# Attention with a gated feed-forward layer: four score banks for the first four pairs, and the first weights' high halves rounded on ScalarE

## The chip, the cores and the metric

The program runs on one NeuronCore of a Trainium2 chip. The metric is the device time of one execution, in microseconds (us); the median of three runs of the kernel before is 751.47 us (749.72 to 752.3). TensorE (PE in the profile) multiplies matrices into PSUM, VectorE (DVE), ScalarE (ACT) and GpSimd (POOL) work on vectors, and SyncE (SP) issues the transfers. Each engine takes its instructions in the order in which they stand in its own queue.

## The reference

Causal attention of 4 batches, 8 heads, 576 tokens and 64 dimensions per head is mixed with a linear memory. Its output, 2304 tokens of 512 features, goes through a gated feed-forward layer ("experts" in the kernel) with 1536 hidden features:

```python
scores = scale * np.matmul(q, k.transpose(0, 1, 3, 2))
scores = np.where(causal, -1000000000.0, scores)
a = softmax(scores);  local = np.matmul(a, v)
q_p = phi(q)                                  # elu(q) + 1
mem_out = (q_p @ M_prev) / (q_p @ z_prev + 1e-6)
attn = g * mem_out + (1 - g) * local          # g: a gate for each head
x = attn.transpose(0, 2, 1, 3).reshape(2304, 512)
out = (silu(x @ w_gate) * (x @ w_val)) @ w_out
```

The weights come as 64-bit floats; everything is asked for in 32-bit precision.

## The kernel before

The 32 pairs of batch and head are handled two heads at a time: 16 "pairs", four to a batch. A pair's `load` brings q and k, `split` parts each into a rounded high half and the rest (`qh`, `ql`, `kh`, `kl`), and a score tile is the sum of three matmul products of these. `scores(t, ...)` makes the tile of 128 queries number t (0 to 3) against the 128(t+1) keys before them, for both heads, one PSUM bank for each head; `scores4` makes the last 64 queries of both heads in two halves of 288 keys, one bank each. From a bank VectorE takes the masked, scaled copy and the row minimum in one instruction (L406, L428), ScalarE the exponential and its sum (L410, L433), GpSimd divides (`weighed`, L449), TensorE transposes (L473, L493), VectorE and ScalarE in turn copy the transposes out (L318, L320), TensorE multiplies with the values (L548, L602) and adds the memory's part (L463, L464), and `give` (L518, L519) writes the pair's features as a high and a low half, which L630 stores to a scratch array in DRAM, `xdh` and `xdl`. The first five pairs (`PLAIN`) keep the attention weights and the values in plain 32 bits, without halves.

PSUM has eight banks here: two for scores (`s`), three for transposes (`tr`), one for the products with values (`av`), one (`g`) and one (`m`) for the experts. `rot` hands out the buffers of a name in turn. Before the two matmul series of a tile write their banks, they wait until the last reader of the second bank is done (L402).

The experts' weights are 12 groups f of 128 hidden features, each in thirds (gate, value, out) of 128 x 512. For each third `weights` loads the raw 64-bit words (L170, two buffers in turn for the first groups), turns them into 32-bit floats in four instructions (L176 on ScalarE, L177, L179, L180 on VectorE; one buffer each for the results `e` and `a`), rounds the high half `wh` (L184 on ScalarE for the groups with the tag "b", L107 on GpSimd for those with the tag "a"), and takes the low half `wl` as the difference (L111, on GpSimd for "a"). Groups 0 to 3, tag "a", are 12 thirds; they are converted beside the first pairs. The other eight groups have the tag "b" and come later.

`moe1` multiplies the first 1536 tokens with groups 0 to 3, 256 tokens at a time, beside the attention of pairs 4 to 15. It loads a slice of `xdh` and `xdl` (L193, L194), which needs the four pairs of a batch stored. What is left is done after the attention, by L203, L212 to L214, L737 to L744.

The code gives each step a priority, and a scheduler places every instruction in its engine's queue by these priorities and by its own estimate of when the operands are there. So an edit of buffers or engines also moves instructions that it does not name. In the first stretch the code gives the steps of pair n and of pair n-1 in the order of `STEPS`.

Of the kernel before, what the change touches and what calls it, by code (L numbers as in the profile page):

```python
# [9 lines left out]
F32 = mybir.dt.float32  # L10
# [28 lines left out]


PLAIN = tuple(range(0, 5))
EV = (1, 2)
P_X = -400
ORDER = (4, 5, 0, 1, 2, 3)
HI_ACT = ('b',)
ACT_K = (0, 1)
N4 = 1
ON_POOL = ("wa", "q", "k")
PS_S, PS_T, PS_A, PS_G, PS_M = 2, 3, 1, 1, 1
# [11 lines left out]
def attention_moe(ctx: ExitStack, tc: tile.TileContext, qt, kt_, v, m, beta, wg, wv, wo, out):  # L61
# [5 lines left out]
    psS = ctx.enter_context(tc.tile_pool(name="psS", bufs=1, space=PSUM))  # L67
# [27 lines left out]
    def rot(pool, name, shape, dtype, n):  # L95
        held = slots.setdefault(name, [0, []])
        if len(held[1]) < n:
            held[1].append(pool.tile(shape, dtype, name=f"{name}{len(held[1])}"))
        held[0] += 1
        return held[1][(held[0] - 1) % n]  # L100
# [160 lines left out]
    with tc.tile_pool(name="sb", bufs=1, reuse_waits="tile") as sb:  # L261
# [48 lines left out]
                SP.dma_start(mm[rows, :, j, :], m[b, rows])  # L310
            return mm

        turn = [0]

        def evac(dst, src):
            turn[0] += 1
# [7 lines left out]
        class Pair:  # L324
# [62 lines left out]
            def scores(self, t, c):  # L387

                w = 128 * (t + 1)
                mx = self.mx  # L390
                ps = [rot(psS, "s", [128, 512], F32, PS_S) for _ in range(2)]
                last = None
                for i, (q, k) in enumerate(self.products):
                    for h in range(2):
                        rows = slice(h * 64, h * 64 + 64)
                        mm = PE.matmul(  # L396
                            ps[h][:, 0:w], q[rows, t * 128 : t * 128 + 128], k[rows, 0:w], start=(i == 0), stop=(i == 2)
                        )
                        if last is not None:
                            follow(mm, last, "the two heads' products take turns")  # L400
                        elif id(ps[1]) in read:
                            follow(mm, read[id(ps[1])], "once both banks are read", mybir.DependencyClass.Sync)  # L402
                        last = mm
                for h in range(2):
                    p = rot(sb, "pl", [128, 512], F32, NBIG) if t > 1 else rot(sb, "ps", [128, 256], F32, NSMALL)
                    read[id(ps[h])] = DVE.tensor_tensor_reduce(  # L406
                        out=p[:, 0:w], in0=ps[h][:, 0:w], in1=maskp[:, 512 - w : 512], op0=ALU.add, op1=ALU.min,
                        scale=-SCALE, scalar=BIG, accum_out=mx[:, c + h : c + h + 1],
                    )
                    ACT.activation(  # L410
                        p[:, 0:w], p[:, 0:w], AF.Exp, bias=mx[:, c + h : c + h + 1], scale=-1.0,
                        accum_out=self.sm[:, c + h : c + h + 1],
                    )
                    self.pts[(t, h)] = p

            def scores4(self):
# [4 lines left out]
                p = p4s[self.n % N4]  # L421
                mx = self.mx
                for half in range(2):
                    ps = rot(psS, "s", [128, 512], F32, PS_S)
                    sl = slice(half * 288, half * 288 + 288)
                    for i, (q, k) in enumerate(self.products):
                        PE.matmul(ps[:, 0:288], q[:, 512:640], k[:, sl], start=(i == 0), stop=(i == 2))
                    read[id(ps)] = DVE.tensor_tensor_reduce(  # L428
                        out=p[:, sl], in0=ps[:, 0:288], in1=mask4 if half else maskp[:, 0:288], op0=ALU.add, op1=ALU.min,
                        scale=-SCALE, scalar=BIG if half == 0 else mx[:, c : c + 1],  # L430
                        accum_out=mx[:, c + half : c + half + 1],
                    )
# [376 lines left out]
```

## Time and profile before

| | us |
|---|---|
| median of three runs | 751.47 |
| the profiled execution | 753.47 |
| its span, first to last instruction | 751.7 |
| TensorE busy | 693.1 (92%) |
| VectorE busy | 401.7 (53%) |
| ScalarE busy | 332.4 (44%) |
| GpSimd busy | 197.9 (26%) |
| mean clock that TensorE was granted | 0.966 |

The profile gives, for groups of instructions by line, how long they took, how long their engine stood idle just before them and what ended that idle time; a view by stretches of the span gives each engine's busy time and TensorE's granted clock; a timeline shows single instructions, with the idle time before each and what ended it in square brackets. The shares over the whole span say little about single stages: TensorE is nearly always busy after the first 125 us, GpSimd is idle after the attention. Line numbers are those of the kernel before; in the changed kernel they are higher by one from `WIDE` on and by seven from `evac` on (L396 is L403 there, L184 is L185).

### The profile page before, as it was taken

To read this page: it belongs to the slowest core of one execution; us is meant where nothing else is said; L and a number is where in the kernel's file an instruction comes from. 1 tells how busy PE (TensorE), PEld (TensorE's weight loads), DVE (VectorE), ACT (ScalarE), POOL (GpSimd) and SP (SyncE) were. 2 spreads that over 40 slices of the span, in tenths; PEclk is the share of its full clock that TensorE was granted. 3 is DMA by queue.
4 is the path that set the end of the run, shared out by engine and by line. 5 is a ranking of instruction groups with operands and counts; after the bars stand their busy time and mean duration, and the time that the engine had idled before them with its cause. 6 is when DMAs were issued, how large, how long until landed. Compare 5 with 4: busy or idle time off the path is not lost.

```text
span 751.7 us, 11326 instructions
## 1 busy us (share of the span) xinstructions
PE 693.1 (92%) x4172; PEld 621.6 (83%) x4172; DVE 401.7 (53%) x1042; ACT 332.4 (44%) x737; POOL 197.9 (26%) x264
## 2 busy tenths in 40 slices
PE   4577798999979999899969999999999999999997
PEld 2466676998769997698859999999999999999996
DVE  8887764776876977775736995111111221211212
ACT  5555455667668686576725663211121111111111
POOL 5885943544444553452300000000000000000000
PEclk9789799999989999899988999999999999999999
DMA  9555144230362312401048760300040310400201
GB/s 262 180 169 148 54 124 150 70 114 19 104 197 88 114 39 78 162 33 61 20 156 295 221 226 26 115 1 1 13 156 1 112 57 0 169 1 1 84 1 43
DMA packets 43928, 72.58 MB, mean 97 GB/s; under 512 B 11744, under 2 KB 24544, under 8 KB 43872
## 3 DMA queue, kind: packets, MB, share of 16 engines
q1 hardware_dynamic: 43728, 71.56, 29.4%
q8 instruction: 33, 0.54, 0.3%
q10 hardware_dynamic: 144, 0.29, 0.1%
q14 instruction: 23, 0.19, 0.1%
HBM read 54.54 MB, written 17.30 MB: 96 GB/s over the span
## 4 chain that ended last, share of the span: by engine, by line
PE 70%; DVE 11%; DMA 8%; ACT 6%; issue 2%; POOL 2%; SPq 0%; DVEq 0%; ACTq 0%; POOLq 0%
PE s L203 13%; PE g L203 9%; PE m L203 8%; PE av L203 6%; PE tr L213 5%; PE tr L212 5%; PE tr L214 5%; PE s L396 3%; PE av L616 2%; PE tr L473 2%; DMA xbl<-xdl 2%; PE av L602 2%; PE m L212 2%; DMA xbh<-xdh 1%; PE m L213 1%
## 5 line engine op out<-in xcount | busy, mean ns | idle before, releaser
L743 ACT CAST uh<-u 128x384 fp32r<-128x384 f32 x56 | 28.8, 514 | 109.8 <-DVE u L738 109.8
L213 PE MATMUL tr<-wl,uh 128*128 128x512 f32 x168 | 66.5, 396 | 0.0
L212 PE MATMUL tr<-wh,uh 128*128 128x512 f32 x168 | 66.1, 393 | 0.0
L214 PE MATMUL tr<-wh,ul 128*128 128x512 f32 x168 | 64.7, 396 | 0.0
L738 DVE SCALAR_TENSOR_TENSOR u<-s,u 128x384 f32<-128x384 f32 x23 | 12.8, 557 | 86.9 <-PE s L203 86.9
L396 PE MATMUL s<-kh,qh 64*128 64x128 f32 (+3 forms) x128 | 31.1, 463 | 28.8 <-DVE mx L406 15.2
L410 ACT ACTIVATE pl<-pl,mx 128x384 f32<-128x384 f32 (+1 forms) x64 | 42.6, 667 | 31.3 <-DVE mx L406 31.2
L449 POOL TENSOR_SCALAR pl<-pl,rs 128x384 f32<-128x384 f32 (+1 forms) x64 | 44.4, 712 | 19.9 <-ACT x L500 10.8
L396 PEld LDWEIGHTS s<-kh,qh 64*128 64x128 f32 x128 | 14.0, 207 | 40.3 <-DVE mx L406 18.6
L111 DVE TENSOR_TENSOR ul<-u,uh 128x384 fp32r<-128x384 f32 x56 | 31.2, 557 | 26.7 <-ACT uh L743 26.7
L111 DVE TENSOR_TENSOR g2l<-tr,g2h 128x512 fp32r<-128x512 f32 (+1 forms) x66 | 36.2, 572 | 17.1 <-ACT g2h L455 16.4
L449 POOL TENSOR_SCALAR ps<-ps,rs 128x128 f32<-128x128 f32 (+1 forms) x64 | 27.9, 454 | 61.2 <-DVE rs L446 26.4
L473 PE MATMUL tr<-ident,pl 128*128 128x128 f32 x224 | 39.9, 316 | 3.5 <-POOL pl L449 2.0
L406 DVE CUSTOM_DVE_ANT_0 pl<-s,maskp 128x384 f32<-128x384 f32 (+1 forms) x64 | 37.7, 618 | 9.9 <-PE s L396 9.9
L473 PEld LDWEIGHTS tr<-ident,pl 128*128 128x128 f32 x224 | 29.3, 161 | 10.4 <-POOL pl L449 4.5
L214 PEld LDWEIGHTS tr<-wh,ul 128*128 128x128 f32 x168 | 31.6, 188 | 7.3
L203 PE MATMUL s<-xbh,wh 128*128 128x384 f32 x92 | 32.1, 352 | 4.9 <-DMA xbh<-xdh 4.9
L212 PEld LDWEIGHTS tr<-wh,uh 128*128 128x128 f32 x168 | 31.6, 188 | 5.2
L213 PEld LDWEIGHTS tr<-wl,uh 128*128 128x128 f32 x168 | 31.6, 188 | 5.1
L410 ACT ACTIVATE ps<-ps,mx 128x128 f32<-128x128 f32 (+1 forms) x64 | 28.9, 452 | 13.3 <-DVE mx L406 13.1
L455 ACT CAST g2h<-tr 128x512 fp32r<-128x512 f32 (+1 forms) x66 | 30.5, 494 | 7.0 <-PE tr L473 4.8
L737 ACT ACTIVATE u<-s 128x384 f32<-128x384 f32 x23 | 11.2, 489 | 49.5 <-PE s L203 49.5
(197 smaller groups left out, 2188.2 us busy)
## 6 DMA issues: line engine op xcount, KB each, us to landing
qr<-in_qt_dram SPq DMA_DIRECT2D x16, 384.0 KB, 4.2
out_dram<-pt SPq DMA_DIRECT2D x18, 256.0 KB, 2.2
kr<-in_kt_dram SPq DMA_DIRECT2D x15, 288.0 KB, 3.8
xdh<-xh SPq DMA_DIRECT2D x15, 288.0 KB, 2.6
xdl<-xl SPq DMA_DIRECT2D x15, 288.0 KB, 2.2
wrawb<-in_wg_dram SPq DMA_DIRECT2D x8, 512.0 KB, 4.1
wrawb<-in_wv_dram SPq DMA_DIRECT2D x8, 512.0 KB, 4.4
wrawb<-in_wo_dram SPq DMA_DIRECT2D x8, 512.0 KB, 4.3
```

The lines of the kernel that those rows point to most:

```text
L111: return eng.tensor_tensor(dst, src, hi.bitcast(F32), op=ALU.subtract)
L203: PE.matmul(ps, wt[:, c], xx[:, kk, :], start=(n == 0), stop=(n == 11))
L212: PE.matmul(ps, uh, hi[:, 1024:1536], start=first, stop=False)
L213: PE.matmul(ps, uh, lo[:, 1024:1536], start=False, stop=False)
L214: PE.matmul(ps, ul, hi[:, 1024:1536], start=False, stop=last)
L396: mm = PE.matmul(ps[h][:, 0:w], q[rows, t * 128 : t * 128 + 128], k[rows, 0:w], start=(i == 0), stop=(i == 2))
L406: read[id(ps[h])] = DVE.tensor_tensor_reduce(out=p[:, 0:w], in0=ps[h][:, 0:w], in1=maskp[:, 512 - w : 512], op0=ALU.add, op1=ALU.min, scal ...
L410: ACT.activation(p[:, 0:w], p[:, 0:w], AF.Exp, bias=mx[:, c + h : c + h + 1], scale=-1.0, accum_out=self.sm[:, c + h : c + h + 1],)
L449: POOL.tensor_scalar(p, p, rs[:, i : i + 1], 1.0, op0=ALU.mult, op1=ALU.mult)
L455: ACT.copy(view(g[0]), src)
L473: PE.transpose(tr[:, c * 128 : c * 128 + 128], p[:, (k0 + c) * 128 : (k0 + c) * 128 + 128], ident)
L743: ACT.copy(uh, u)
```

## The change

```diff
+WIDE = 4
...
-HI_ACT = ('b',)
+HI_ACT = ('a', 'b')
...
-        turn = [0]
+        turn, wide = [0], [0]
+
+        def score_bank(n):
+            wide[0] += 1
+            if n < WIDE and (wide[0] - 1) % 4 > 1:
+                return rot(psG, "g", [128, 512], F32, PS_G) if wide[0] % 4 else rot(psM, "m", [128, 512], F32, PS_M)
+            return rot(psS, "s", [128, 512], F32, PS_S)
...
-                ps = [rot(psS, "s", [128, 512], F32, PS_S) for _ in range(2)]
+                ps = [score_bank(self.n) for _ in range(2)]
...
-                    ps = rot(psS, "s", [128, 512], F32, PS_S)
+                    ps = score_bank(self.n)
```

The ten banks that a pair's scores ask for go round s, s, g, m in pairs 0 to 3, and stay s, s from pair 4 on. The high halves of the 12 first thirds of weights are rounded by ScalarE's L184 instead of GpSimd's L107. No instruction is added or taken away.

The queues change with it. On TensorE, where pair 0's last scores end and pair 1's first begin (`kh0`, `qh0` are pair 0's halves, `kh1`, `qh1` pair 1's), there stood:

```order
L427 MATMUL s1_171<-kh0_144,qh0_142 128x288
L427 MATMUL s1_171<-kl0_145,qh0_142 128x288
L427 MATMUL s1_171<-kh0_144,ql0_143 128x288
L396 MATMUL s0_170<-kh1_233,qh1_231 128x128
L396 MATMUL s1_171<-kh1_233,qh1_231 128x128
```

and now there stands:

```order
L434 MATMUL s1_171<-kh0_144,qh0_142 128x288
L434 MATMUL s1_171<-kl0_145,qh0_142 128x288
L434 MATMUL s1_171<-kh0_144,ql0_143 128x288
L403 MATMUL g0_184<-kh1_235,qh1_233 128x128
L403 MATMUL m0_185<-kh1_235,qh1_233 128x128
```

Pair 1's first tile now goes to the experts' banks. Its second tile goes back to the two `s` banks.

On GpSimd, between the division of pair 0's first two tiles (`ps`) and that of its later ones (`pl`), there stood the following. `waa`, `wh`, `wl` belong to the weights, `vs` to the values of pairs 5 and 6, and `qh0`, `kh0`, `ql0`, `kl0` by then to pair 2:

```order
L107 TENSOR_SCALAR wh0_505<-waa0_512 128x512
L111 TENSOR_TENSOR wl0_506<-waa0_512,wh0_505 128x512
L107 TENSOR_SCALAR vs0_982<-vp0_980 128x2x5x64
L107 TENSOR_SCALAR vs1_1180<-vp1_1178 128x2x5x64
L107 TENSOR_SCALAR wh0_505<-waa0_512 128x512
L111 TENSOR_TENSOR wl0_506<-waa0_512,wh0_505 128x512
L107 TENSOR_SCALAR qh0_142<-qr0_125 128x640
L107 TENSOR_SCALAR kh0_144<-kr0_126 128x576
L111 TENSOR_TENSOR ql0_143<-qr0_125,qh0_142 128x640
L111 TENSOR_TENSOR kl0_145<-kr0_126,kh0_144 128x576
L107 TENSOR_SCALAR wh0_505<-waa0_512 128x512
L449 TENSOR_SCALAR pl0_202<-pl0_202,rs1_317 128x384
```

and now there stands:

```order
L112 TENSOR_TENSOR wl0_508<-waa0_514,wh0_507 128x512
L108 TENSOR_SCALAR qh0_142<-qr0_125 128x640
L108 TENSOR_SCALAR kh0_144<-kr0_126 128x576
L112 TENSOR_TENSOR ql0_143<-qr0_125,qh0_142 128x640
L108 TENSOR_SCALAR vs0_984<-vp0_982 128x2x5x64
L112 TENSOR_TENSOR kl0_145<-kr0_126,kh0_144 128x576
L108 TENSOR_SCALAR vs1_1180<-vp1_1178 128x2x5x64
L456 TENSOR_SCALAR pl0_204<-pl0_204,rs1_319 128x384
```

Three roundings of weights and one low half no longer stand ahead of the division. Over the whole queue, 12 low halves stood ahead of the last division of pair 3 before, and 8 now.

On ScalarE, ahead of the second and last rounding of pair 3's features (`xh1_442`, now `xh1_444`), there stood:

```order
L410 ACTIVATE ps3_193,sm0_169<-ps3_193,mx0_168 128x256
L410 ACTIVATE pl2_214,sm0_169<-pl2_214,mx0_168 128x384
L410 ACTIVATE pl3_217,sm0_169<-pl3_217,mx0_168 128x384
L410 ACTIVATE pl4_357,sm0_169<-pl4_357,mx0_168 128x512
L518 CAST xh1_442<-av0_275 128x320
```

and now there stands:

```order
L417 ACTIVATE pl3_219,sm0_169<-pl3_219,mx0_168 128x384
L177 ACTIVATE wea0_511<-wrawa1_519 128x512
L185 CAST wh3_872<-waa0_514 128x512 x2
L366 ACTIVATE ph0_158<-qr0_125 128x640
L417 ACTIVATE pl4_359,sm0_169<-pl4_359,mx0_168 128x512
L525 CAST xh1_444<-av0_277 128x320
```

The roundings of the last two thirds of weights (`wh3`, twice) now stand in that queue ahead of pair 3's last rounding. On VectorE, ahead of pair 4's first tile of 512 keys (`pl4`) and a few rows ahead of the low half of those features, there stood the scaling of the memory's part (`w`, `mem`):

```order
L377 TENSOR_SCALAR w0_263<-tr0_249 128x6
L378 RECIPROCAL w0_263<-w0_263 128x6
L379 TENSOR_TENSOR w0_263<-w0_263,gx_108 128x6
L382 TENSOR_TENSOR mem1_291<-tr0_249,w0_263 128x384
L406 ISA pl4_357,mx0_168<-s0_170,maskp_94 128x512
```

and now there stand the last two thirds of weights (`wea`, `waa`), one behind the other; before, all twelve conversions stood further ahead of pair 3's end:

```order
L181 SCALAR_TENSOR_TENSOR waa0_514<-wrawa0_509,waa0_514 128x512
L178 TENSOR_SCALAR wea0_511<-wea0_511 128x512
L180 TENSOR_SCALAR waa0_514<-wea0_511 128x512
L181 SCALAR_TENSOR_TENSOR waa0_514<-wrawa1_519,waa0_514 128x512
L413 ISA pl4_359,mx0_168<-s0_170,maskp_94 128x512
```

The third of these rows writes the one buffer `waa`, from which GpSimd must have taken the low half of the third before.

On SyncE the loads of raw weights stand later against the pairs' stores. The last one (`wo` of group 3) stood before pair 2's store and now stands just ahead of pair 3's. The load of pair 8's q, which stood behind the four loads of `xdh` and `xdl` for the experts, now stands between the two of `xdh` and the two of `xdl`.

## The prediction

> **What bounds the kernel now.** I read the slices of the span first, to find the stretches in which TensorE is not the limit.
>
> ```profile
> PE   4577798999979999899969999999999999999997
> DVE  8887764776876977775736995111111221211212
> PEclk9789799999989999899988999999999999999999
> ```
>
> A slice is 18.8 us. Over the first six, some 112 us, TensorE has gaps and VectorE works at seven or eight tenths; later TensorE is near nine tenths or above, and the few dips stand where a batch ends. The stretches in numbers (columns: length, then busy time of PE, its weight loads, DVE, ACT, POOL, then the granted clock):
>
> ```profile
> 14.00:112.00 98.00, 76.35 (x445) 59.85 (x446) 75.30 (x214) 51.57 (x132) 71.78 (x85) 0.88 0.45 143
> 125.00:752.00 627.00, 603.13 (x3645) 550.79 (x3641) 307.42 (x778) 267.87 (x573) 110.79 (x152) 0.98 0.25 83
> ```
>
> From 125 us on TensorE is busy 603.13 of 627 us (96%). The change takes no matmul away, so nothing is to be had there. From 14 to 112 us no engine is full: TensorE is idle for 98 - 76.35 = 21.7 us, VectorE for 98 - 75.30 = 22.7, and they idle in turn. That stretch sets when the first experts can start, as the chain that ended last shows between 109 and 118 us:
>
> ```profile
> 109.94 2.08 DMA xdh<-xh
> 112.10 5.17 DMA xbh<-xdh
> 117.31 0.58 PE g L203
> ```
>
> Pair 3's store at 109.94 closes the first batch, the experts' load follows it, and TensorE's first expert matmul follows the load. All that makes the store earlier moves the start of the 96% stretch by as much. The prediction is a prediction of that store.
>
> What ends the idle time from 14 to 112 us, in the view of waits (us in total, times, longest):
>
> ```profile
> PE s L396 <- DVE mx L406: 7.4, 5, 4.0
> DVE pl L406 <- PE s L396: 6.8, 5, 3.6
> PE s L396 <- DVE mx L428: 6.5, 1, 6.5
> DVE waa L179 <- POOL wl L111: 5.3, 3, 2.3
> PE s L427 <- DVE mx L406: 4.2, 2, 2.5
> DVE xl L111 <- ACT xh L518: 2.5, 2, 1.3
> DVE rs L442 <- ACT ps L410: 2.4, 3, 0.8
> PE tr L473 <- POOL pl L449: 2.0, 1, 2.0
> DVE w L377 <- PE tr L368: 1.5, 1, 1.5
> DVE ps L406 <- PE s L396: 1.3, 2, 1.0
> DVE rs L442 <- ACT p L433: 1.0, 1, 1.0
> ```
>
> Of TensorE's 21.7 us, 7.4 + 6.5 + 4.2 = 18.1 are waits until a score bank has been read. Much of that isn't lost by the banks, though: in the longest one VectorE was itself full.
>
> ```profile
> 24.00:30.50 6.50, 0.02 (x2) 0.02 (x2) 6.50 (x13) 1.71 (x4) 6.48 (x5) 0.83 0.51 173
> 30.48 0.48 PE L396 MATMUL s<-kh,qh 64*128 64x128 f32 x2 [6.51 <-DVE mx L428]
> ```
>
> VectorE was busy for all 6.50 us, so another bank wouldn't have shortened its queue. What the banks can win is only VectorE's own idle time; the 18.1 us are no gain by themselves.
>
> **The change part by part.** (a) *Score banks.* Four banks let TensorE write the next tile while VectorE still reads the last. VectorE then finds its scores ready: 6.8 + 1.3 = 8.1 us of its idle time end with a score matmul. One of them is out of reach:
>
> ```profile
> 108.06 0.69 DVE L406 CUSTOM_DVE_ANT_0 pl<-s,maskp 128x512 f32<-128x512 f32 x1 [3.63 <-PE s L396]
> 102.68 4.43 PE L602 MATMUL av<-g,vz 128*128 128x320 f32 x20
> ```
>
> At 104 to 108 us it waits for pair 4, which keeps two banks, behind value products on which TensorE is busy. That leaves 8.1 - 3.6 = 4.5 us; the ends are 0 and 8.1, and I take 4.5, since each of these waits begins right behind a bank wait of TensorE. What is late next is the division by GpSimd (2.0 us in the list).
>
> (b) *Roundings of weights.* Twelve instructions go from GpSimd to ScalarE:
>
> ```profile
> L107 POOL TENSOR_SCALAR wh<-waa 128x512 fp32r<-128x512 f32 x12 | 8.5, 711 | 9.6 <-DVE waa L180 7.6 <-DVE w L378 1.3 <-DVE w L377 0.7
> L184 ACT CAST wh<-wab 128x512 fp32r<-128x512 f32 x24 | 14.7, 617 | 1.0 <-DVE wab L180 0.7
> L111 POOL TENSOR_TENSOR wl<-waa,wh 128x512 fp32r<-128x512 f32 x12 | 16.0, 1331 | 0.7
> ```
>
> GpSimd loses 12 x 0.711 = 8.5 us of its 71.78; ScalarE gets 12 x 0.617 = 7.4 us, by the same rounding of the later weights, and goes from 51.57 to 59 of 98 us, still the least loaded; that is hidden as long as the cast doesn't wait in front of other work. For one third the way to the low half gets shorter by 0.711 - 0.617 = 0.09 us, next to nothing; what counts is that GpSimd's queue is shorter when the low half's turn comes. VectorE's three waits for it (5.3 us) lie between 0 and 5.3 afterwards; I take half, a gain of 2.6, because the order leaves the low half behind five divisions in several places still.
>
> (c) *VectorE beside GpSimd.* Two instructions of the same stretch:
>
> ```profile
> 46.85 1.96 POOL L111 TENSOR_TENSOR ql<-qr,qh 128x640 fp32r<-128x640 f32 x1
> 47.34 1.50 DVE L442 SCALAR_TENSOR_TENSOR rs<-sm,oy 128x5 f32<-128x5 f32 x1
> L442 DVE SCALAR_TENSOR_TENSOR rs<-sm,oy 128x5 f32<-128x5 f32 x4 | 3.5, 883 | 1.0 <-ACT p L433 1.0
> L442 DVE SCALAR_TENSOR_TENSOR rs<-sm,oy 128x4 f32<-128x4 f32 x5 | 0.8, 162 | 2.4 <-ACT ps L410 2.4
> ```
>
> Five numbers a lane took 1.50 us, and ended as GpSimd's instruction did, while four take 0.162 elsewhere. So VectorE loses 4 x (0.883 - 0.162) = 2.9 us in this group alone. GpSimd's share that goes is 8.5 / 71.78 = 12%: 0.3 us of these 2.9, and I put 0.5 for all groups (ends 0 and 2.9). The Trainium skill's page "SBUF — State Buffer", section "Who interferes with whom", says that a VectorE instruction with two SBUF inputs and a GpSimd instruction that reads SBUF shut each other out for their whole length, and that ScalarE waits for no one. The trace agrees (1.50 against 0.162 us). By that rule alone each of the twelve roundings could hold VectorE for up to its 0.711 us, and this term would be up to 8.5 in place of 0.5.
>
> (d) *Other waits of VectorE*, for ScalarE's exponentials and copies and for the memory's products: 2.5 + 2.4 + 1.5 + 1.0 = 7.4 us. With scores of the next pair at hand the scheduler has put them between; I count a third, 2.5 (ends 0 and 7.4).
>
> (e) *What is added.* The cast waits for L180, and behind it in ScalarE's queue stand exponentials, copies and pair 3's rounding. The worst place is the end of pair 3: the last third's L179 waits for the low half of the third before, its cast stands before pair 3's rounding. From the end of the last but one L180 that takes the cast, the low half, L179, L180 and the cast again,
>
> ```profile
> L180 DVE SCALAR_TENSOR_TENSOR waa<-wrawa,waa 128x512 int32<-128x512 int32 x12 | 9.6, 798 | 0.0
> L179 DVE TENSOR_SCALAR waa<-wea 128x512 int32<-128x512 int32 x12 | 7.3, 610 | 5.4 <-POOL wl L111 5.3
> ```
>
> 0.617 + 1.331 + 0.610 + 0.798 + 0.617 = 4.0 us. TensorE's value products (4.43 us above) run beside it, so between 0 and 4.0 of it are lost; I take 2.0. The last raw load stands just ahead of pair 3's store on SyncE, but its buffer is free two thirds earlier, so it costs nothing; it would hold the store if that buffer were late.
>
> (f) *SyncE's order.* Pair 8's q goes ahead of the experts' low half:
>
> ```profile
> 110.00:117.30 7.30, 4.01 (x31) 3.12 (x29) 6.72 (x21) 4.57 (x13) 6.63 (x7) 0.98 0.69 225
> qr<-in_qt_dram SPq DMA_DIRECT2D x16, 384.0 KB, 4.2
> ```
>
> 384 KB at 225 GB/s are 1.7 us; TensorE has pair 4's work until the low half is asked for, so 0 to 1.7, and I take 0.5. The three low halves of group 3 that now come after pair 3's end cost 3 x 1.331 = 4 us on GpSimd; TensorE needs group 3 only behind 60 expert matmuls, with pair 4's work between them, and that covers it.
>
> The sum: 4.5 + 2.6 + 0.5 + 2.5 - 2.0 - 0.5 = **7.6 us earlier**. The profiled execution took 753.47 us (span 751.7 and 1.8 around it), so it would take 745.9; the median of the three runs, 751.47, lies 2.0 lower, which gives **743.9**.
>
> **The rivals.** *B, VectorE's queue is the bound and only the place of the waits moves.* For it speaks the stretch 24 to 30.5 us. Only (a) is won, and (e) is paid in full: 4.5 - 4.0 = 0.5 us, 751.0. If the scheduler's new order undid the banks, the time would be the same; against that stands the order, in which `g` and `m` do alternate with `s`.
>
> *C, the weights' chain becomes the bound: slower.* Each third now crosses VectorE, ScalarE, GpSimd and VectorE again, in strict queues. Three of twelve waited for the low half before, 5.3 / 3 = 1.8 us each. If all twelve wait so, that is 21.2 - 5.3 = 15.9 us lost, against 4.5 + 0.5 + 2.5 - 2.5 = 5.0 won: 751.47 + 10.9 = 762.4. It decides from a mean wait of (5.3 + 5.0) / 12 = 0.86 us on. Against it: ScalarE is idle nearly half the time.
>
> *D, more is won.* All of (b) and (d) go: 4.5 + 5.3 + 0.5 + 7.4 - 2.5 = 15.2, so 736.3. VectorE's 22.7 us leave room for it, but every wait would have to be filled.
>
> *E, TensorE's clock.* After the 6.5 us gap the granted clock is 0.73, after another of 4.0 us 0.55, and with 8.28 of 8.50 us busy it is 1.00:
>
> ```profile
> 30.50:45.20 14.70, 11.66 (x62) 8.73 (x63) 11.18 (x36) 8.68 (x24) 11.63 (x16) 0.73 0.39 136
> 78.30:87.20 8.90, 7.88 (x39) 6.00 (x40) 6.48 (x22) 5.24 (x16) 8.53 (x12) 0.55 0.12 39
> 87.20:95.70 8.50, 8.28 (x56) 6.85 (x55) 5.70 (x17) 3.69 (x9) 7.03 (x9) 1.00 0.05 10
> ```
>
> If four banks broke the work into short bursts, and the clock stood at 0.55 throughout, TensorE's 76.35 us would become 76.35 x 0.88 / 0.55 = 122, which is 24 us more than the stretch: 775. The rows speak for the opposite: fewer long gaps, a higher clock. The Trainium skill's page "TensorE: Matmul & The Clock Gate", section "A second HAM failure mode: psum-queue depth-cycling", speaks against this change: it reports a kernel whose cycling through PSUM banks made short pauses and let the clock fall again and again. The rows above have the low clock behind gaps of 6.5 and 4.0 us, and the full one where TensorE is busy.
>
> **How the numbers follow.** The forecast has 0.68, B 0.15, C 0.08, D 0.07, E 0.02. Some 0.3% (2.3 us) is what a measurement of this kernel tells from no change: faster 0.68 + 0.07 = 0.75, same 0.15, slower 0.10. The bounds of (a) to (f) would let the forecast lie between -22.7, all of VectorE's idle time, and +5.7, where nothing is won and (e) and (f) cost all. The range takes in B and the forecast with the larger part of (b) and (d) or none of them, 738.0 to 752.0, and leaves out D, C and E, 0.17.
>
> **What would show it.** Right: pair 3's store near 102 us; the waits of score matmuls for VectorE's row minimum from 18.1 us to under 6; VectorE above 80% up to that store; TensorE's clock above 0.88 there; the casts of weights near 0.62 us; all later stretches as before, shifted. Wrong: VectorE waiting for the low half more than 5.3 us in all, or ScalarE in front of its casts (C); the store early but the first expert matmul not, through the load of q or group 3; an end that does not follow the store.

## The result and the profile after

The changed kernel takes **732.75 us** (median of four runs, 730.8 to 733.51), the kernel before 751.67 (four runs on the same chip, 749.72 to 752.3): ratio 0.9749, 95% interval 0.9721 to 0.9776, or 18.9 us less. The forecast was 7.6 us less, 743.9 us; the measured time lies below its range.

The slices of the span of the changed kernel (18.3 us each):

```profile
PE   4699879999899998999989999999999999999997
DVE  8999756777786797866629993111121211211212
PEclk9899999999899999999999999999999999999999
```

VectorE now stands at nine tenths in slices 2 to 4, where it stood at seven and eight, and the granted clock dips less. The stretch from 14 us until pair 3's store has landed, and all from 125 us on (length, busy time of PE, its weight loads, DVE, ACT, POOL, clock):

```profile
14.00:97.00 83.00, 72.12 (x442) 57.39 (x443) 74.90 (x222) 57.59 (x149) 65.84 (x73) 0.94 0.51 166
125.00:731.50 606.50, 589.39 (x3532) 536.81 (x3531) 300.97 (x751) 258.64 (x554) 104.24 (x142) 0.99 0.25 84
```

VectorE is busy as long as before (74.90 against 75.30 us) in a stretch that is 15 us shorter: its idle time fell from 22.7 to 8.1 us. TensorE's fell from 21.7 to 10.9. The store and what follows it on SyncE's queue, in the timeline:

```profile
95.11 0.33 SPq L637 DMA_DIRECT2D xdh<-xh  x1
...
97.25 0.54 SPq L194 DMA_DIRECT2D xbh<-xdh  x1
```

Pair 3's store comes at 95.11 in place of 109.94, **14.8 us** earlier, and the load of the experts' features follows 2.1 us behind, as before. The waits of VectorE in the same stretch (us in total, times, longest), then TensorE's three longest:

```profile
DVE wea L178 <- ACT wea L177: 2.3, 1, 2.3
DVE waa L180 <- POOL wl L112: 2.2, 3, 1.6
DVE g L325 <- ACT g L327: 0.8, 1, 0.8
DVE rs L449 <- ACT ps L417: 0.7, 1, 0.7
...
DVE rs L449 <- ACT p L440: 0.3, 1, 0.3
...
DVE w L384 <- PE tr L375: 0.2, 1, 0.2
```

```profile
PE s L403 <- DVE mx L413: 5.5, 2, 3.4
PE g L403 <- DVE mx L413: 1.8, 1, 1.8
PE av L555 <- DVE xl L112: 1.8, 1, 1.8
```

No wait of VectorE for a score matmul is left among them; there were 8.1 us. TensorE's waits for score banks fell from 18.1 to 7.3. The longest of VectorE's, the 3.6 us for pair 4's tile of 512 keys, went like this:

```profile
86.83 4.44 PE L609 MATMUL av<-g,vz 128*128 128x320 f32 x20
...
91.20 0.50 PE L403 MATMUL s<-kh,qh 64*128 64x512 f32 x2
...
91.62 0.43 DVE L180 TENSOR_SCALAR waa<-wea 128x512 int32<-128x512 int32 x1 [1.60 <-POOL wl L112]
92.08 0.69 DVE L181 SCALAR_TENSOR_TENSOR waa<-wrawa,waa 128x512 int32<-128x512 int32 x1
92.69 0.68 DVE L413 CUSTOM_DVE_ANT_0 pl<-s,maskp 128x512 f32<-128x512 f32 x1
```

TensorE still makes this tile behind 4.4 us of value products, as before. But VectorE now has the last two thirds of weights to convert meanwhile, with 1.6 us of waiting for a low half among them, and finds the tile ready at 92.69.

### The profile page after: what moved, and what is told of

Its sections match the earlier page's. It is cut to its first block, busy times and chain, and to the rows that moved or that the text cites. A ratio compares the mean times of both kernels' runs of the same rounds, so it can differ in the third digit from the quotient of the medians.

```text
span 731.5 us, 11320 instructions
## 1 busy us (share of the span) xinstructions
PE 690.9 (94%) x4172; PEld 619.4 (85%) x4172; DVE 400.7 (55%) x1042; ACT 337.3 (46%) x749; POOL 193.6 (26%) x252
## 4 chain that ended last, share of the span: by engine, by line
PE 71%; DVE 12%; DMA 6%; ACT 4%; issue 3%; POOL 3%; DVEq 0%; SPq 0%; ACTq 0%; POOLq 0%
PE s L204 13%; PE g L204 10%; PE m L204 9%; PE av L204 6%; PE tr L214 5%; PE tr L213 5%; PE tr L215 5%; PE s L403 3%; PE tr L480 3%; PE av L623 2%; DMA xbl<-xdl 2%; DMA xbh<-xdh 1%; PE m L213 1%; DVE ph L367 1%; DVE waa L181 1%
## 5 line engine op out<-in xcount | busy, mean ns | idle before, releaser
L456 POOL TENSOR_SCALAR pl<-pl,rs 128x384 f32<-128x384 f32 (+1 forms) x64 | 45.1, 721 | 18.9 <-ACT x L507 12.2
L403 PE MATMUL s<-kh,qh 64*128 64x128 f32 (+3 forms) x112 | 25.8, 438 | 16.6 <-DVE mx L413 9.2
L413 DVE CUSTOM_DVE_ANT_0 pl<-s,maskp 128x384 f32<-128x384 f32 (+1 forms) x56 | 33.0, 617 | 9.2 <-PE s L403 9.0
L417 ACT ACTIVATE ps<-ps,mx 128x128 f32<-128x128 f32 (+1 forms) x64 | 28.8, 452 | 10.4 <-DVE mx L413 10.3
L204 PE MATMUL s<-xbl,wh 128*128 128x384 f32 x92 | 31.7, 344 | 1.7 <-DMA xbl<-xdl 1.7
L403 PEld LDWEIGHTS s<-kh,qh 64*128 64x128 f32 x112 | 11.7, 195 | 25.4 <-DVE mx L413 10.9
```

The costliest lines, as they stand in the source:

```text
L204: PE.matmul(ps, wt[:, c], xx[:, kk, :], start=(n == 0), stop=(n == 11))
L403: mm = PE.matmul(ps[h][:, 0:w], q[rows, t * 128 : t * 128 + 128], k[rows, 0:w], start=(i == 0), stop=(i == 2))
L413: read[id(ps[h])] = DVE.tensor_tensor_reduce(out=p[:, 0:w], in0=ps[h][:, 0:w], in1=maskp[:, 512 - w : 512], op0=ALU.add, op1=ALU.min, scal ...
L417: ACT.activation(p[:, 0:w], p[:, 0:w], AF.Exp, bias=mx[:, c + h : c + h + 1], scale=-1.0, accum_out=self.sm[:, c + h : c + h + 1],)
L456: POOL.tensor_scalar(p, p, rs[:, i : i + 1], 1.0, op0=ALU.mult, op1=ALU.mult)
```

## The experiments

All runs compute the whole reference. In the table, "us" is the median, "store" is the start of pair 3's store in the profiled execution, "behind" the span less that, "end" TensorE's wait at the attention's end for the load (`xbh`) of the first features that are multiplied behind it. Ratios are to runs of the kernel before on the same chip; the runs were made on several chips, on which that kernel took 751.7 to 754.0 us, so between rows a difference of 1 or 2 us is better read from the ratios.

| run | us | ratio, 95% interval | store | behind | end |
|---|---|---|---|---|---|
| before | 751.67 | | 109.9 | 641.8 | 4.9 |
| the change | 732.75 | 0.9749 [0.9721, 0.9776] | 95.1 | 636.4 | 0.3 |
| e1 banks only | 725.17 | 0.9629 [0.9598, 0.9661] | 92.4 | 632.9 | 0 |
| e2 roundings only | 747.01 | 0.9919 [0.9888, 0.9950] | 112.5 | 633.2 | 0 |
| e3 late order | 754.73 | 1.0016 [0.9988, 1.0044] | 110.3 | 641.4 | 5.0 |
| e4 roundings on VectorE | 732.07 | 0.9716 [0.9668, 0.9765] | 97.2 | 634.7 | 0.6 |
| e5 banks, old order | 752.64 | 0.9994 [0.9979, 1.0009] | 111.2 | 640.0 | 5.0 |
| e6 roundings on ScalarE, e1's order | 726.62 | 0.9649 [0.9629, 0.9668] | 91.1 | 633.8 | 0.3 |
| e7 roundings on GpSimd, the change's order | 733.89 | 0.9751 [0.9725, 0.9778] | 98.4 | 638.2 | 0.5 |
| e8 four banks for pair 4 too | 730.05 | 0.9697 [0.9676, 0.9718] | 95.2 | 631.5 | 3.8 |
| e9 new order, then old | 741.27 | 0.9846 [0.9818, 0.9874] | 91.8 | 647.8 | 4.9 |
| e10 old order, then new | 742.58 | 0.9879 [0.9846, 0.9912] | 109.7 | 636.6 | 0.2 |
| e11 old order on three engines | 756.79 | 1.0045 [1.0026, 1.0064] | 110.2 | 641.1 | 4.9 |
| e12 old order on GpSimd | 752.25 | 0.9982 [0.9959, 1.0005] | 110.3 | 640.1 | 4.1 |
| e13 two banks, new order on GpSimd | 740.58 | 0.9837 [0.9805, 0.9869] | 101.5 | 637.3 | 0 |
| e14 halves of q, k early | 751.75 | 0.9978 [0.9954, 1.0002] | 114.6 | 630.8 | 2.0 |
| e15 halves of q, k late | 742.42 | 0.9857 [0.9826, 0.9887] | 91.4 | 649.2 | 0.8 |
| e16 copies to ScalarE | 735.96 | 0.9782 [0.9749, 0.9814] | 90.5 | 643.3 | 4.8 |
| e17 divisions early | 753.52 | 0.9988 [0.9966, 1.0010] | 94.4 | 654.5 | 4.9 |
| e18 new end | 748.27 | 0.9926 [0.9899, 0.9954] | 109.8 | 636.5 | 0.2 |

The last three columns are of one execution each. That of e14 ran 747.15 us, the fastest of its 12 and 4.6 below their median; e11's and e17's lie 3.6 and 2.8 below theirs, e10's and e7's 5.5 and 4.5 above, the slowest of their six. So the "behind" of these five rows is off by some such amount.

### One part of the change at a time

```diff
 e1: the banks alone
-HI_ACT = ('a', 'b')
+HI_ACT = ('b',)
 e2: the roundings alone
-WIDE = 4
+WIDE = 0
 e4: the first roundings on VectorE instead
-                ACT.copy(hi[:, c], a.bitcast(F32))
+                DVE.tensor_scalar(hi[:, c], a.bitcast(F32), 1.0, 0.0, op0=ALU.mult, op1=ALU.add) if tag == "a" else ACT.copy(hi[:, c], a.bitcast(F32))
 e3: the kernel before, with twelve expert matmuls and the last store of part put later
+                if f == 0 and j == 1 and t0 == NT1 - N1:
+                    follow(mm, pairs[NP - 1].acr, "the last experts' products fill the end of the attention")
...
+            if j == 1 and t0 == NT1 - N1:
+                follow(st, pairs[NP - 1].stored, "the last pair's store goes first")
```

> Four banks for the first four pairs, the first weights' high halves rounded on GpSimd as before the change. Theory 1, VectorE's idle time up to pair 3's store is what was won, and most of it by the banks: the store of pair 3 at 99 to 103 us (before 109.94, after 95.11), VectorE's waits for score matmuls from 8.1 us to under 1.5, time 736 to 742 us. Theory 2, the freed GpSimd won it and the banks only let TensorE run ahead of a full VectorE: store at 106 us or later, time 746 us or more.

> Two score banks as before, the high halves on ScalarE as after. Theory 1: store of pair 3 at 105 to 109 us, VectorE still waits 5 us or more for score matmuls, time 744 to 750 us, part of it from the order at the end of the attention, where 18 expert matmuls stand behind pair 15's first transposes of the memory's part (0 before, 12 after). Theory 2: store at 100 us or earlier, time 741 us or less.

> The kernel before, with one edit at the end of the attention: the last 12 expert matmuls of the first part stand behind pair 15's first transposes of the memory's part, and their store behind pair 15's. Nothing earlier moves. The change won 14.8 us up to pair 3's store and 20.2 us in all. Theory 3, some 3 of the other 5.4 us are matmuls that fill TensorE's gap while pair 15's features go through DRAM: TensorE busy about 14 us in place of 11.1 in the 17 us from pair 15's first store on, time 748 to 749.5 us. Rival, the later gain is a phase of the clock or of the queues that follows the early shift: no difference, 751 to 752 us.

> The changed kernel with the twelve roundings on VectorE in place of ScalarE, so GpSimd is as free as after the change and VectorE has 12 more instructions of 0.42 to 0.70 us. Theory 1, up to pair 3's store VectorE is now nearly full (85.6 us busy of 96.5): the store comes 5 to 8 us later than 95.1, time 738 to 741 us. Rival, the waits of the weights' chain or GpSimd bound it: the chain loses a crossing of engines, store within 2 us of 95.1, time 731 to 735 us.

The banks alone are **faster than the change**, 725.17 us, which is 11 us below the range that I had given; the roundings alone win 6.5 us, and nothing of it at pair 3's store, which is later (112.5) than either theory had it; both together win less than the banks alone. Twelve more roundings on VectorE (e4) cost nothing that can be measured against the change in the whole time, though the store is 2.1 us later. Two things that the prediction rested on are thereby in doubt: that parts have prices which add up, and that VectorE's time sets the store. e3 missed its aim: the wait of 5.0 us that it was to fill is still there, since the moved matmuls ran ahead of the store in question and not behind it, so it says nothing of that wait. e18 repeats it better.

All these edits also let the scheduler make new queues. The next runs part the two.

### The order held still

A table now gives the queues. Each instruction of an engine is put behind the one that stands ahead of it in another built kernel; only the place is given, all waits for data stay as they are.

```diff
+    made = [i for i in nc.cur_bb.bb.instructions if type(i).__name__ not in ("BassTilePoolBoundary", "InstRegisterMove")]
+    order_only = mybir.DependencyInfo(mybir.DependencyClass.NoSync, mybir.DependencyReason.DATA)
+    for packed in ISSUE.values():
...
+        for a, b in zip(seq, seq[1:]):
+            tc.add_manual_dep(made[b], made[a].name, order_only, reason="issue order as given")
 e5: four banks, roundings on GpSimd; ISSUE = all five queues of the kernel before
 e6: e1 with HI_ACT = ('a', 'b'); ISSUE = all queues of e1, without the twelve roundings
 e7: the change with HI_ACT = ('b',); ISSUE = all queues of the change, without the twelve roundings
```

> Four score banks for pairs 0 to 3 and the roundings on GpSimd, as in the kernel that has the banks alone (725.2 us), but every engine's instructions stand in the order that the kernel before had: no instruction is moved on any queue. Theory 'waits': the banks win because the scores stand ready, whatever the order; then term (a) shows alone, 4.5 to 8.1 us, 743 to 748 us where the kernel before takes some 752, and pair 3's store comes at 102 to 106 us. Theory 'order': with the old queues TensorE still reaches the next tile only behind the same work, so nearly nothing is won, 749.5 to 753, the store at 108 to 111; the 26 us of the banks alone are then what the new order wins, which the scheduler can only make with four banks. Rival: the banks alone win most of it in any order, under 738.

> The order of the kernel with the banks alone (725.2 us) on every engine, but the twelve roundings are done by ScalarE; only these twelve are placed by the scheduler. TensorE, VectorE and SyncE have not one instruction moved. If the roundings on ScalarE cost by themselves (their wait for VectorE holds exponentials and copies behind them), the time is that of the change, 730 to 734 us. If they cost only through the other order that the scheduler then makes for all engines, 723.5 to 727.

> The mirror image: the order of the changed kernel (732.7 us) on every engine, but the twelve roundings stay on GpSimd, and only they are placed by the scheduler. If the roundings cost by themselves: 724 to 728 us, like the banks alone. If the order does it: 731 to 734.5, and if GpSimd was the better of the two only where the order was made for it, up to 738.

With the old queues the four banks win **nothing**: ratio 0.9994. The waits of TensorE in e5 from 14 to 112 us:

```profile
PE s L403 <- DVE mx L435: 5.8, 1, 5.8
PE tr L480 <- POOL pl L456: 4.7, 3, 2.0
PE tr L500 <- POOL ps L456: 2.5, 1, 2.5
PE tr L375 <- DVE g L325: 2.3, 1, 2.3
PE av L555 <- DVE xl L112: 2.2, 1, 2.2
PE g L403 <- DVE mx L413: 1.6, 1, 1.6
PE s L403 <- DVE mx L413: 1.3, 2, 1.1
PE tr L500 <- DVE g L325: 0.9, 1, 0.9
PE av L555 <- DVE g L325: 0.8, 1, 0.8
```

The waits for score banks are down from 18.1 to 5.8 + 1.6 + 1.3 = 8.7 us, and the others (transposes behind GpSimd's divisions, products behind copies) make up 13.4 in their place, and three smaller ones 1.4 more. The sum is 23.5, as against 18.1 + 3.8 in the kernel before (3.8 are its five smaller waits there, the division's 2.0 among them). TensorE came to the scores earlier, and waited as long at the next rows of its queue. VectorE is as busy as before in the same stretch (75.67 against 75.30 us), and so is the granted clock (0.88). Its waits for scores fell from 8.1 to 6.1 us only, and those for low halves rose from 5.3 to 6.7:

```profile
14.00:112.00 98.00, 75.53 (x439) 59.42 (x436) 75.67 (x212) 50.40 (x130) 70.30 (x83) 0.88 0.44 138
```

```profile
DVE waa L180 <- POOL wl L112: 6.7, 4, 2.3
DVE pl L413 <- PE s L403: 4.3, 2, 3.6
...
DVE pl L413 <- PE m L403: 1.8, 2, 1.0
```

The roundings, with everything else held in place, cost 1.4 us by the medians in e1's order (the intervals of the ratios overlap), and 1.1 less than GpSimd's in the change's order. The 7.6 us between e1 and the change are thus not a price of the roundings: their move led the scheduler to other queues.

### Which queue, and which stretch

```diff
 e8:  e1 with WIDE = 5
 e9:  four banks, roundings on GpSimd; ISSUE = e1's queues up to what pair 3's store needs, then the old ones
 e10: the same with old and new exchanged
 e11: ISSUE = the old queues of VectorE, ScalarE and GpSimd; the scheduler places TensorE's and SyncE's
 e12: ISSUE = the old queue of GpSimd alone
 e13: WIDE = 0; ISSUE = e1's queue of GpSimd alone
 e16: e1 with EV = (1, 3): VectorE copies one in three transposes, not one in two
```

> The banks alone, roundings on GpSimd, and four banks for pair 4 as well (its scores are the last before the experts need the banks g and m). Theory: what the scheduler can put in front of the value products is worth more than the bank; pair 4's scores already stood ahead of them in the changed kernel, so little is left, 723 to 727 us. Rival: the first expert matmul waits for pair 4's reads of g and m, 728 to 732.

> Four banks, roundings on GpSimd, issue order given: up to pair 3's store every queue stands as in the kernel with the banks alone (725.2 us, store at 92.4), everything behind it as in the kernel before. Theory 'late order too': of the 27 us between the old order with four banks (752.6) and the new one only the early 18 (store 111.2 to 92.4) are won here, 733 to 737 us; the other 9 come from the order behind the store. Theory 'shift': all that follows starts earlier and gains by itself what the later part shows, 724.5 to 728.

> The mirror image: up to pair 3's store the old order, behind it the order of the kernel with the banks alone. Theory 'late order too': store at 110 to 112 us, and 8 to 10 us are won behind it, 742 to 745. Theory 'shift': 751 to 754, as with the old order throughout.

> Four banks, roundings on GpSimd; VectorE, ScalarE and GpSimd have the old order, TensorE's is left to the scheduler, which may put score products ahead as far as the four banks go. If TensorE's own queue is what the banks set free: 725 to 738 us. If the order in which VectorE reads scores and GpSimd divides is what sets the first batch: 746 to 753, the store at 106 to 111.

> Four banks, roundings on GpSimd; GpSimd alone has the old order (in it pair 2's halves of q and k stand behind two more roundings and two low halves of weights and two copies of values), the other four queues are left to the scheduler. If GpSimd's queue sets the first batch: 742 to 752 us, the store at 102 to 111. If VectorE's and TensorE's do: 724 to 732, the store under 97.

> Two score banks and the roundings on GpSimd, as in the kernel before; GpSimd alone has the order of the kernel with the banks alone, the other queues are left to the scheduler. If GpSimd's order is all that counts and the banks only led the scheduler to it: 724 to 734 us, the store of pair 3 at 92 to 97. If the order needs the banks too (TensorE and VectorE wait for two banks as before): 740 to 753, with TensorE's bank waits at 15 us or more.

> The banks alone (725.2 us), and VectorE copies one in three transposes out of PSUM in place of one in two, ScalarE the others. If VectorE, at 86% up to pair 3's store, is what limits the kernel now: 718 to 723 us. If the order that the scheduler makes is what decides: 724 to 732, in either direction for no reason of the copies themselves.

e9 and e10 win 11.6 and 10.3 us: the new order counts on both sides of the store. e10 is in the range of "late order too". Neither theory of e9 has its number; its time lies above both, because the old queues behind the store took longer (647.8) than where they stood all along (640.0).

e11 took 4 us more than the upper end of the range that it was given. e12 is the sharpest run: **GpSimd's old queue alone takes the whole gain away**, with four banks, and with the other four queues made anew by the scheduler around it. e13 shows the other side. With two banks and GpSimd's new queue the time is 11.9 us less than before, and the store comes at 101.5, half way. The score waits are those of two banks (14 to 103.6 us; 10.6 and one of 1.0 for TensorE, less than the 15 that I had expected):

```profile
PE s L403 <- DVE mx L413: 10.6, 7, 2.7
```

```profile
DVE pl L413 <- PE s L403: 7.6, 5, 3.2
...
DVE ps L413 <- PE s L403: 2.2, 4, 1.0
```

VectorE waits 9.8 us for scores there. In e1, with four banks, one such wait is left up to the store, which is 9.1 us earlier:

```profile
DVE pl L413 <- PE s L403: 0.3, 1, 0.3
```

So with GpSimd's new queue the banks go with some 9 us at the store, and in the old order with nothing. How much of the 9 is the banks' own isn't shown, since the scheduler made the other four queues of e13 for two banks. For the whole gain both were needed in these runs: the banks alone, in the old order, win nothing, and GpSimd's queue, without the banks, wins less than half.

e16 is slower than both of its ranges. Its store comes 1.9 us earlier than in e1, as less work on VectorE would have it, though its queues are new as well; but the end wait of 4.8 us is back, and the stretch behind the store is 10 us longer. e8 has the time of its rival, without the wait that the rival named; its store is 2.8 us later and the end wait is 3.8. What in its order does that was not followed up.

### What in GpSimd's queue

```diff
 e14: ISSUE = GpSimd's old queue, with only qh, ql, kh, kl moved to their places in e1
 e15: ISSUE = e1's queue of GpSimd, with only qh, ql, kh, kl moved to their old places
 e17: ISSUE = GpSimd's old queue, with only the divisions (L456) moved to their places in e1
```

> Four banks; GpSimd's old order, in which only the halves of q and k are moved to the places that they have in the new order; the other queues are left to the scheduler. Theory 'splits': pair 3's halves come at 34 to 37 us in place of 45, scores follow, and most of the 27 us is won, 726 to 735. Rival 'divisions and the rest': the place of the divisions and of the weights counts as much, 738 to 752.

> The mirror image: four banks, GpSimd's new order with only the halves of q and k put back to their old places. Theory 'splits': nearly all is lost, 743 to 753 us. Rival: 725 to 735, since divisions and weights keep their new places.

> Four banks; GpSimd's old order, in which only the divisions by the row sums are moved to the places that they have in the new order (so the halves of q and k and the weights keep their old sequence among themselves); the other queues are left to the scheduler. Theory 'divisions': pair 3's store comes at 91 to 99 us, as with the halves of q and k late (91.4), and TensorE's transposes wait for divisions under 3 us up to there (10.2 with the halves early, 8.2 with the old order of GpSimd). Rival 'the whole order': moving one kind ahead makes another late, the store at 104 to 114. For the whole time, the part behind the store adds 631 to 649 us in the runs so far: 722 to 748 by the theory, 735 to 763 by the rival.

For the store my theory of the halves of q and k fell: moving them ahead made it later than ever (114.6), putting them back left it at 91.4. For the whole time it isn't refuted so clearly: e14 wins nothing, but e15 loses 17 of e1's 27 us, 0.6 short of the theory's range and 7 outside the rival's. The store is held by the divisions: with them alone moved, it comes at 94.4. TensorE's waits for GpSimd's divisions `pl` say why, first e14, then e17 (both 14 to 110 us):

```profile
PE tr L480 <- POOL pl L456: 10.2, 5, 5.5
```

```profile
PE tr L480 <- POOL pl L456: 2.0, 1, 2.0
```

A division that stands behind other work in GpSimd's queue holds the transposes, these the value products, and these the features that are stored. But e17 takes 753.5 us all the same. What it wins at the store it loses behind it (654.5), above the range that I had given: its TensorE has the end wait of 4.9 us and others. An early store alone is no gain. The stores of the next two pairs show where most of it is lost, first e17's, then pair 5's in the kernel before:

```profile
131.31 0.33 SPq L637 DMA_DIRECT2D xdh<-xh  x1
162.72 0.33 SPq L637 DMA_DIRECT2D xdh<-xh  x1
```

```profile
161.82 0.33 SPq L630 DMA_DIRECT2D xdh<-xh  x1
```

| run | pair 3's store | pair 4's | pair 5's | from pair 5's to the end |
|---|---|---|---|---|
| before | 109.9 | 133.9 | 161.8 | 589.9 |
| the change | 95.1 | 117.1 | 146.2 | 585.3 |
| e1 | 92.4 | 118.4 | 143.4 | 581.9 |
| e9 | 91.8 | 123.8 | 151.7 | 587.8 |
| e15 | 91.4 | 124.2 | 154.8 | 585.8 |
| e17 | 94.4 | 131.3 | 162.7 | 586.2 |

By pair 5's store e17 has lost its whole lead of 15.5 us, e15 has kept 7.0 of 18.5, and e9 10.1 of 18.2; e1 and the change have kept theirs. So the place of the divisions moves pair 3's store, but that is not yet a gain in time, and what holds pairs 4 and 5 in these three runs wasn't separated.

### Behind the store

```diff
 e18: four banks, roundings on GpSimd; ISSUE = the old queues up to what pair 14's store needs, then e1's
```

> Four banks, roundings on GpSimd; every queue in the old order until pair 14 is stored, and from there as in the kernel with the banks alone, in which twelve expert matmuls stand behind the last attention matmul of TensorE, while the last features are loaded. The old order with four banks takes 752.6 us; its TensorE waits 4.9 us there and runs at half clock for 10 us. If that one place makes the gain behind the store (the stretch of 17 us there held 11.14 us of matmuls at clock 0.70 before, 13.96 at 0.90 in the changed kernel, 4.8 us more of work): 746 to 749.5 us, the wait under 1.5 us. If the gap only moves, or the load ends later: 751 to 754.

The end of the attention in the kernel before, TensorE's timeline (start, duration, what; in brackets the idle time ahead):

```profile
386.44 0.28 PE L616 MATMUL av<-g2l,vs 128*128 128x64 f32 x1
391.60 1.01 PE L203 MATMUL s<-xbh,wh 128*128 128x384 f32 x2 [4.89 <-DMA xbh<-xdh]
392.41 0.52 PE L203 MATMUL g<-xbh,wh 128*128 128x384 f32 x1
...
399.62 0.52 PE L203 MATMUL s<-xbh,wh 128*128 128x384 f32 x1
399.94 0.52 PE L203 MATMUL s<-xbl,wh 128*128 128x384 f32 x1
...
400.83 0.34 PE L203 MATMUL s<-xbh,wl 128*128 128x384 f32 x1
401.00 0.34 PE L203 MATMUL g<-xbl,wh 128*128 128x384 f32 x1
```

The wait has a tail: until 400 us a matmul takes 0.52 us, and the next one starts 0.32 behind it; then one takes 0.34, and the next starts 0.17 behind it. From 392 to 400 us the granted clock (the third number from the end) is 0.50:

```profile
392.00:400.00 8.00, 7.24 (x23) 6.73 (x23) 0.00 (x0) 1.69 (x2) 0.00 (x0) 0.50 0.77 263
```

The load follows the store of the first part of pair 15's features, here before, in the change and in e18:

```profile
385.06 0.32 SPq L630 DMA_DIRECT2D xdh<-xh  x1
```

```profile
366.08 0.32 SPq L637 DMA_DIRECT2D xdh<-xh  x1
```

```profile
380.40 0.32 SPq L637 DMA_DIRECT2D xdh<-xh  x1
```

From that store to its next wait for `xbh` TensorE has 1.7 us of work before (to 386.7), 6.1 in the change (to 372.2) and 6.5 in e18 (to 386.9), while store and load take 6.5 us (385.06 to 391.60). In e18 twelve expert matmuls stand behind the attention's last ones. The stretches of 17 us, before, in the change and in e18 (columns as above):

```profile
385.00:402.00 17.00, 11.14 (x43) 10.53 (x44) 2.70 (x7) 3.49 (x7) 0.00 (x0) 0.70 0.76 251
```

```profile
366.00:383.00 17.00, 13.96 (x73) 13.07 (x72) 3.82 (x9) 4.28 (x9) 0.00 (x0) 0.90 0.77 260
```

```profile
385.00:402.00 17.00, 14.80 (x71) 13.43 (x70) 6.36 (x14) 7.15 (x12) 0.00 (x0) 0.90 0.89 317
```

e18 has only the last stretch from the new order, and takes 748.27 us: 5.7 less than the kernel before on that chip, 4.4 less than e5. Its wait for `xbh` is 0.2 us, that for `xbl` 2.0, so the 1.5 that I had expected holds for the first alone. In e5 they are 5.0 and 0.7, so 3.5 us less of waiting go with 4.4 us less in all. The last two columns of the table mostly agree: 640 to 655 us behind the store where the wait is 4 us or more, 631 to 638 where it is less. Two runs do not fit: e8, with 631.5 us and a wait of 3.8, and e15, with 649 and 0.8, whose loss lies ahead of pair 5's store, as shown above. So this isn't all that counts there.

## Why the prediction was right in sign and wrong in size

- **What bounds the kernel:** right that the stretch up to 112 us limits, and that TensorE's 18.1 us for score banks are no gain by themselves; in e5 they fall from 18.1 to 8.7, and nothing is won. Wrong was that all that makes pair 3's store earlier moves the rest by as much ("the prediction is a prediction of that store"): e17 has the store 15.5 us earlier and the same time.
- **Step (a), score banks, 4.5 of 8.1:** this is the first step that failed. VectorE's waits for scores up to the store went altogether, 8.1, also the one "out of reach": VectorE now converts weights while TensorE multiplies with the values. And they went for another reason than the step gave. With the old queues four banks take 2.0 us off these waits, and win 0 (e5); with GpSimd's new queue two banks leave 9.8 us of them, four 0.3 (e13 beside e1).
- **Step (d), other waits, a third of 7.4:** the second. Those rows fell to 0.7 + 0.3 + 0.2 = 1.2 us, a gain of 6.2 against 2.5. I had treated the new order as a small side effect; without it nothing is won (e5). At pair 3's store it acts by way of GpSimd's divisions (e12, e14, e17), which the prediction named as "late next" and priced at no more than their 2.0 us; the gain in the whole time isn't traced to them, since e17 wins none.
- **Step (b), roundings, 2.6 of 5.3:** VectorE's wait for the low half fell from 5.3 to 2.2, near the forecast, and the casts took 0.614 us. But that was luck: in e1, with the roundings still on GpSimd, it is 2.6, so the fall came with the new queues. The move by itself is worth nothing that these runs tell, in either order (e6, e7).
- **Step (c), VectorE beside GpSimd, 0.5:** right in that it is small. In e6 GpSimd has 5.6 us less to do than in e1, and VectorE is not faster for it: 0.334 us for one of 206 instructions in e1, 0.335 for one of 209 in e6 (14 to 93 us, e1, then e6):

```profile
14.00:93.00 79.00, 67.95 (x438) 54.27 (x435) 68.83 (x206) 49.10 (x130) 63.51 (x79) 0.96 0.52 166
```

```profile
14.00:93.00 79.00, 68.06 (x441) 54.55 (x439) 70.02 (x209) 55.36 (x142) 57.96 (x69) 0.96 0.55 170
```

  By the rule of the Trainium skill's page "SBUF — State Buffer", section "Who interferes with whom", up to 8.5 us would have been VectorE's gain, by the prediction's estimate; no such gain shows.
- **Step (e), the chain at pair 3's end, -2.0:** the wait for the low half that the step described is there, 1.6 us at 91.62, and is counted under (b). Besides, VectorE waits 2.3 us for ScalarE's `wea` (0.4 before) and 0.8 for a copy, which the step had not named: 2.7 us more. So the size is near, and the place is another. e6, with the casts on ScalarE, has the store no later than e1.
- **Step (f), SyncE's order, -0.5:** not separated by a run. The low half's load is issued 3.8 us behind `xbh`'s in the change, 3.0 before.
- **"All later stretches as before, shifted":** the third step that failed. Behind the store the change is 641.8 - 636.4 = 5.4 us shorter, and e18 finds 4.4 to 5.7 us at the last batch's end alone, where the change has TensorE's wait covered.

In sum, VectorE's waits give 8.1 + 3.1 + 6.2 - 2.7 = 14.7 us. Since VectorE is as long busy as before, this must come near the 14.8 measured at the store, whatever the cause; it sorts the gain by the prediction's steps and doesn't explain it. 14.8 and the 5.4 behind the store make 20.2, the difference of the two spans. **Rival D** (15.2 us, 736.3) came near the store's size, in part by luck: it had 4.5 for (a) and all 5.3 and 7.4 of (b) and (d), where 8.1, 3.1 and 6.2 went, and nothing behind the store. Still its 0.07 was too little: I had discounted each wait by how it looked in the old queues. B and C did not happen, though e5 is what B's second clause says, the old order's waits in another place. Of E the opposite happened: the clock of the first stretch rose from 0.88 to 0.94 in the change. In e5, with four banks in turn and the old queues, it stayed at 0.88, so the banks neither raise nor lower it by themselves. The loss from cycling through PSUM banks that the Trainium skill's page "TensorE: Matmul & The Clock Gate", section "A second HAM failure mode: psum-queue depth-cycling", reports of another kernel thus doesn't show here.

Open: which divisions matter most, what holds pairs 4 and 5 in e9, e15 and e17, and why the scheduler's queues with the roundings moved are worse by 7.6 us than without.

## What to carry to other kernels

Where a scheduler makes the queues, a buffer's worth is the order that it allows: build the edit, hold the order still in one run and the edit in another, before putting a price on either. Removing a wait of one engine only counts if the next row of its queue is ready; look at which engine feeds that row, here GpSimd with its divisions. A milestone that comes earlier, like pair 3's store, is a gain only if the next ones come earlier too. And when a change has two parts, time each alone: here one part alone was 7.6 us better than both.

## What the runs showed of the hardware

- A TensorE wait of 4.9 us cost more than itself: behind it matmuls of 128x384 started 0.32 us apart in place of 0.17 for some 8.5 us, at a granted clock of 0.50. With 3.5 us less of waiting there e18 took 4.4 us less than e5.
- Twelve instructions of 0.711 us (their mean in the kernel before) taken off GpSimd beside a VectorE that is 87% busy made VectorE no faster (68.83 us for 206 instructions in e1, 70.02 for 209 in e6).
- The same work in other orders of the queues took from 725 to 757 us, with the same banks, the same division of the work among the engines and the same 4172 matmuls (e1, e11).
